# Attention weights turned in pairs of 64-row tiles, eight blocks a visit, with the first scores head by head

## The chip, the cores and the metric

The kernel runs on one core of a Trainium2 chip. The metric is the device time of one execution in microseconds (us), lower is better. The engines speak here by their names in the profile: PE (TensorE, the matmul array) with PEld (its weight loads), DVE (VectorE), ACT (ScalarE), POOL and SP (the queue that issues most DMA).

## The reference

Three stages over 4 batch entries of 576 positions and 512 features, all float32.

```python
def _attn_ref(q, k, v):              # (4, 8, 576, 64): 8 heads of 64
    q_rot, k_rot = rotate(q), rotate(k)
    scores = q_rot @ k_rot.T / np.sqrt(64)
    attn = np.exp(scores - scores.max(-1, keepdims=True))
    attn = attn / (attn.sum(-1, keepdims=True) + 1e-9)
    return attn @ v
def _moe_ref(x, g_ln, w_ch1, w_ch2): # 512 -> 2048 -> 512
    xn = (x - mu) / np.sqrt(var + 1e-6) * g_ln
    return x + np.maximum(xn @ w_ch1, 0) @ w_ch2
def _moe2_ref(x, w_in, g_ln, w_sg, b_sg, w_out):
    u, v = split(gelu(x @ w_in))     # 512 -> 1024
    v_s = w_sg @ layernorm(v) * ... + b_sg    # mixes the 576 positions
    return x + (u * v_s) @ w_out
```

## The kernel before

**Groups, blocks, units.** A group is one batch entry (g = 0 to 3). A block is a pair of heads (p = 0 to 3) of a group and a part `hi` of its query positions: `hi` = 0 holds 384 of them, `hi` = 1 the other 192. A unit is up to 128 query positions of a block: three full units for `hi` = 0; one full unit and one single unit of 64 positions for `hi` = 1 (`PARTS`, L20). Group 0 takes the four blocks of `hi` = 0 first and then the four of `hi` = 1; the other groups alternate.

**One unit** (`Attn.unit`, L258). Scores S for 576 keys go into two PSUM areas, S[0] and S[1], one a head, two banks each. In a full unit head j lies on array rows 64j to 64j+63, so the two heads' matmuls (K = 64, 288 columns, L271) use different row halves of the array. A single unit has both heads' 64 queries side by side as 128 (tile `qd`), with all 128 rows. DVE takes the row maxima (L293), ACT the exp with its sum (L303) into the tile P (128 queries by 1152 keys of both heads).

**Turning P** (`turn`, L317, and `evac`, L340). P is needed with keys on partitions, so blocks of 128 by 128 are transposed by the array (L334), three to a visit, into one of two PSUM tiles T of one bank each, and copied to the SBUF tile PT by ACT or DVE (L347; L352 and L356 for a single unit). Which of the two copies is decided when the program is built (L343, with `EVEN`). A full unit has 9 blocks, a single one 5.

**P V** (`values`, L382). When all of a block's PT stands, chunk 4 of the keys (64 keys of each head in one zero-padded 128-row tile) goes over the full array (L394), then chunks 0 to 3 head by head in column halves (64 array columns each, L398). It takes a T tile; the reciprocal sums, spread by `scale` (L364), are transposed into another (L408). ACT copies P V to the tile x0 (L410), and DVE multiplies (L415, L419).

**LayerNorm and MLP.** `ln` (L491) and `rest` (L517) run when all four pairs of a half (group 0) or of a group are there; group 0 normalises half 0 and half 1 apart. `ln` has its mean's matmul in a T tile (L508), `rest` its variance's in an MLP bank (L549; for groups 1 to 3 with 64 of the columns of `ones`, so that both halves lie in one tile). The MLP steps `up` (L644) and `down` (L671) have six matmuls of 288 columns each and use two more PSUM banks (`mps`, counted by `mpsb`). Weights come as doubles and are split by `convert` (L614) on ACT and DVE during group 0. For half 0 alone, `group0` (L732) offers four up and four down steps of pass 0 and two up steps of pass 1. After the MLP of group 3 the second block, `moe2` (L895), runs; no line of it changes.

**The order** of each engine's work is written out when the program is built: `Sched` (L64) keeps a clock for each engine, asks every task when its next step can start and how long the step takes, takes the earliest start and among equals the lowest rank (`RANK`, `UNIT`, `NORM`, `REST`); a task of lower rank that can start within `HOLD` of the chosen step's length goes ahead of it (L100). The MLP has rank 5. The numbers of this planner decide the order only; the waits are semaphores.

Of the kernel before, what the change touches and what calls it, by code (L numbers as in the profile page):

```python
# [15 lines left out]
HQ = 288  # L16
# [47 lines left out]
class Sched:  # L64
# [7 lines left out]
    def __init__(self):  # L72
        self.e = dict.fromkeys(("PE", "DVE", "ACT", "POOL", "SP"), 0.0)
        self.tasks = []
        self.n = 0

# [6 lines left out]
    def go_on(self, t, end):  # L83
        try:
            t["eng"], t["at"], t["us"], *rank = t["gen"].send(end)
# [6 lines left out]
    def run(self, until=lambda: False):  # L92
        while self.tasks and not until():
# [41 lines left out]
class Attn:  # L135
# [10 lines left out]
    def __init__(self, tc, ctx, k, groups, sched):  # L146
# [5 lines left out]
        self.T, self.qin, self.kin, self.vfree, self.K = Bank(2), Bank(QB), Bank(2), Bank(2), Bank(KB)  # L152
# [105 lines left out]
    def unit(self, i):  # L258
# [3 lines left out]
        x0 = (g, B["p"])  # L262

        heads = range(2 if m == 128 else 1)
        for n in range(2):
            yield "PE", (lambda: latest(*self.Sfree, Kb["k"], B["q"], self.k["x0_free"](*x0))) if n == 0 else 0.0, 0.57
# [5 lines left out]
            self.Sfree = [None, None]  # L272
        e = c.e["PE"]
        if u["t"] == 0:
            self.k["x0"](*x0)
        if u["last"]:
            self.qin.give(B["qslot"], e + 0.1)
            if B["hi"]:
                self.QD.give(B["dslot"], e + 0.1)
            Kb["kusers"] -= 1  # L280
            if Kb["kusers"] == 0:
                self.K.give(Kb["kslot"], e + 0.1)
        if i + 1 < len(self.units):
            c.task(self.unit(i + 1), UNIT[self.units[i + 1]["g"]])
        if u["t"] == 0:
            self.ahead(B["n"])
            B["su"] = self.p.tile([128, 6], F32, tag="su", name="su", bufs=3)
            B["left"] = 0
        at = []
        nb = self.p.tile([128, 2], F32, tag="nb", name="nb", bufs=3)  # L290
        for j in heads:
            e = yield "DVE", e + 0.35 if j == 0 else 0.0, 0.77
            nc.vector.tensor_reduce(nb[:, j:j + 1], S[j], AX.XY, ALU.max, negate=True)  # L293
            at.append(e + 0.1)
        P = None
        u["P"] = []
        for j in heads:
            e = yield "ACT", (lambda: latest(at[0], self.P.free())) if j == 0 else at[j], 0.97
            if j == 0:
                slot = self.P.take()  # L300
# [5 lines left out]
            if len(heads) == 1:  # L306
                self.Sfree[1] = e + 0.05
# [823 lines left out]
```

## Time and profile before

| | |
|---|---|
| median of 3 runs | 948.84 us (948.66 to 951.78) |
| the profiled execution | 947.07 us, its span 945.3 us |
| PE busy | 916.1 us (97%) |
| DVE, ACT busy | 638.3 us (68%), 490.9 us (52%) |
| granted PE clock | 9 or more tenths in all slices |

The page gives each engine's busy time, and digits for 40 equal slices of the span (23.6 us each; a digit is the busy share in tenths, 9 is 90% or more). Matmuls overlap on PE, so the sum of their durations is more than its time; the distance between starts tells what one costs. In the timeline a row is: start, time until the end of the last of the merged instructions, engine, line, operation, out<-in, rows*columns of the array used, shape of the moving operand, and count. A float32 matmul appears as two instructions, a transpose as one.

### The profile page before, as it was taken

Reading aid. Unit: us, or ns where it says so; the run is one execution under the profiler, and the core shown is the slowest. Engines: PE = TensorE matmul, PEld = TensorE weight load, DVE = VectorE, ACT = ScalarE, POOL = GpSimd, SP = SyncE. Lnnn points to the kernel's source line nnn. Section 1 sums busy time; section 2 is a strip of 40 time slices with the busy share of each in tenths; the row PEclk is TensorE's granted clock in tenths of the full one; section 3 lists DMA queues with packets and bytes.
Section 4 is the critical chain, followed back from the end, with each engine's and each line's share of the span. In section 5 each row is a group of like instructions: output and inputs, shape, how many; then the busy total and the mean of one; then the engine's idle time right before and its main releaser. Section 6 shows DMA issues by size and latency. Waiting matters only on the chain.

```text
span 945.3 us, 16622 instructions
## 1 busy us (share of the span) xinstructions
PE 916.1 (97%) x6448; PEld 799.5 (85%) x6448; DVE 638.3 (68%) x1353; ACT 490.9 (52%) x1191; POOL 0.8 (0%) x9
## 2 busy tenths in 40 slices
PE   4889999999999999999999999989999999999998
PEld 2446878788788787899877899989999999999998
DVE  6799887887869744825767423674534898676754
ACT  2688787778654755524255413444322656263530
POOL 0000000000000000000000000000000000000000
PEclk9999999999999999999999999999999999999999
DMA  6477616674536055225730453878752201202011
GB/s 205 167 239 242 218 43 199 220 249 172 201 110 206 18 182 182 84 74 184 230 114 22 131 163 98 304 238 295 247 190 80 84 1 31 83 1 88 1 51 51
DMA packets 57791, 134.69 MB, mean 142 GB/s; under 512 B 8048, under 2 KB 30448, under 8 KB 57712
## 3 DMA queue, kind: packets, MB, share of 16 engines
q1 hardware_dynamic: 56880, 132.96, 42.5%
q8 instruction: 51, 0.84, 0.4%
q10 hardware_dynamic: 832, 0.66, 0.3%
q14 instruction: 28, 0.23, 0.1%
HBM read 106.50 MB, written 26.21 MB: 140 GB/s over the span
## 4 chain that ended last, share of the span: by engine, by line
PE 93%; DVE 3%; ACT 2%; DMA 1%; issue 1%; SPq 0%; DVEq 0%
PE S L271 9%; PE T L334 8%; PE m L686 7%; PE m L685 7%; PE m L687 7%; PE m L655 7%; PE PV L398 7%; PE m L656 7%; PE m L657 7%; PE PV L394 2%; PE p L964 2%; PE p L962 2%; PE p L963 2%; PE p L1062 2%; PE p L1046 2%; PE p L1061 2%
## 5 line engine op out<-in xcount | busy, mean ns | idle before, releaser
L655 PE MATMUL m<-xh,w 128*128 128x288 f32 x480 | 147.1, 306 | 3.5 <-DVE h L665 3.5
L685 PE MATMUL m<-h,w 128*128 128x288 f32 x480 | 146.0, 304 | 0.0
L686 PE MATMUL m<-h,w 128*128 128x288 f32 x480 | 141.8, 295 | 0.0
L656 PE MATMUL m<-xl,w 128*128 128x288 f32 x480 | 141.6, 295 | 0.0
L657 PE MATMUL m<-xh,w 128*128 128x288 f32 x480 | 141.2, 294 | 0.0
L687 PE MATMUL m<-h,w 128*128 128x288 f32 x480 | 140.5, 293 | 0.0
L303 ACT ACTIVATE P<-S,nb 128x576 f32<-128x576 f32 x144 | 106.4, 744 | 42.4 <-DVE nb L293 39.3
L665 DVE SCALAR_TENSOR_TENSOR h<-m,h 128x288 fp32r<-128x288 f32 x128 | 58.1, 455 | 100.5 <-ACT h L663 99.4
L293 DVE TENSOR_REDUCE nb<-S 128x1 f32<-128x576 f32 x144 | 103.6, 752 | 26.4 <-PE S L271 25.8
L334 PE MATMUL T<-ident,P 128*128 128x128 f32 x656 | 100.1, 280 | 9.0 <-ACT P L303 4.9
L347 ACT COPY PT<-T 128x384 f32<-128x384 f32 x157 | 70.7, 483 | 69.4 <-PE T L334 69.2
L334 PEld LDWEIGHTS T<-ident,P 128*128 128x128 f32 x656 | 74.9, 141 | 37.3 <-issue 12.7
L663 ACT ACTIVATE h<-m 128x288 fp32r<-128x288 f32 x128 | 52.5, 410 | 100.2 <-PE m L657 98.7
L271 PE MATMUL S<-K,qin 64*128 64x288 f32 x512 | 85.2, 439 | 11.0 <-DVE K L205 11.0
L655 PEld LDWEIGHTS m<-xh,w 128*128 128x128 f32 x480 | 90.1, 188 | 5.8 <-DVE h L665 4.2
L685 PEld LDWEIGHTS m<-h,w 128*128 128x128 f32 x480 | 90.1, 188 | 0.8 <-DVE acc L709 0.4
L686 PEld LDWEIGHTS m<-h,w 128*128 128x128 f32 x480 | 90.4, 188 | 0.4
L656 PEld LDWEIGHTS m<-xl,w 128*128 128x128 f32 x480 | 90.3, 188 | 0.2
L657 PEld LDWEIGHTS m<-xh,w 128*128 128x128 f32 x480 | 90.3, 188 | 0.0
L687 PEld LDWEIGHTS m<-h,w 128*128 128x128 f32 x480 | 90.1, 188 | 0.0
L271 PEld LDWEIGHTS S<-K,qin 64*128 64x128 f32 x512 | 47.7, 190 | 31.1 <-DVE K L205 11.0
L398 PE MATMUL PV<-PT,vin 128*64 128x384 f32 (+1 forms) x512 | 70.3, 413 | 0.0
(148 smaller groups left out, 1797.3 us busy)
## 6 DMA issues: line engine op xcount, KB each, us to landing
w<-wsc SPq DMA_DIRECT2D x96, 512.0 KB, 4.0
cd<-in_w SPq DMA_DIRECT2D x32, 512.0 KB, 4.3
wsc<-w SPq DMA_DIRECT2D x24, 512.0 KB, 4.2
kin<-in_k SPq DMA_DIRECT2D x15, 576.0 KB, 5.9
vin<-in_v SPq DMA_DIRECT2D x20, 320.0 KB, 3.9
qin<-in_q SPq DMA_DIRECT2D x16, 384.0 KB, 5.2
x1d<-x SPq DMA_DIRECT2D x32, 144.0 KB, 3.3
x<-x1d SPq DMA_DIRECT2D x32, 144.0 KB, 2.8
```

Of the source, the lines that this page charges most:

```text
L271: nc.tensor.matmul(S[j][:, n, :], q, Kb["K"][r, a:a + HQ], start=True, stop=True)
L293: nc.vector.tensor_reduce(nb[:, j:j + 1], S[j], AX.XY, ALU.max, negate=True)
L303: nc.scalar.activation(P[:, 576 * j:576 * j + 576].rearrange("p (n k) -> p n k", n=2), S[j], AF.Exp, bias=nb[:, j:j + 1], scale=1.0, accum ...
L334: nc.tensor.transpose(ps[:, 128 * n:128 * n + 128], P[:, 128 * i:128 * i + 128], self.k["ident"])
L347: copy(t[:, 3 * k:3 * k + 3, q0:q0 + 128], ps[:, 0:384].rearrange("p (c q) -> p c q", c=3))
L398: nc.tensor.matmul(ps[r, 0:n], V["vin"][:, ch, r], t[:, 5 * j + ch, 0:n], start=False, stop=ch == 3, skip_group_check=True)
L655: nc.tensor.matmul(ps, w[:, 0, ms], xh[:, kc, :], start=kc == 0, stop=False)
L656: nc.tensor.matmul(ps, w[:, 0, ms], xl[:, kc, :], start=False, stop=False)
L657: nc.tensor.matmul(ps, w[:, 1, ms], xh[:, kc, :], start=False, stop=kc == 3)
L685: nc.tensor.matmul(ps, w[:, 0, ms], t[:, 0, :], start=a == 0, stop=False)
L686: nc.tensor.matmul(ps, w[:, 1, ms], t[:, 0, :], start=False, stop=False)
L687: nc.tensor.matmul(ps, w[:, 0, ms], t[:, 1, :], start=False, stop=a == n - 1)
```

## The change

`turn` becomes a task of a whole block: it goes through all 128 by 128 blocks of P of the block's units, eight to a visit (in group 0's `hi` = 0 blocks four or five). A block of P is turned by two transposes, of rows 0 to 63 and 64 to 127, each 64 columns wide, in different row halves of the array and into different banks. T becomes one tile of two banks. `evac` copies each unit's part of a visit in one instruction. `values` takes all chunks in column halves, chunk 4 too, each with its own head's 64 columns of V; P V and the reciprocals lie in the two banks of one T tile, or for group 0's `hi` = 0 in two of the MLP's banks. There too the heads of a unit are tasks of their own in `unit`, and the chunks of P V are single steps. The variance's matmul in `rest` uses all 128 columns of `ones`. `Sched` knows three modes of PE (full, "r" for row tiles, "c" for column tiles) and adds 0.2 to a step that changes the mode, after having chosen it. The ranks and `EVEN` have new numbers.

```diff
-UNIT = [2, 1, 3, 2.5]
-EVEN = [0, 9, 3, -1]
-RANK = dict(turn=4.5, evac=1.25, values=2.25, end=-1, convert=2.75, prep=3.5, load=4, loader=4)
-NORM, REST = [2.25, 0, 3.5, 1.25], [0.25, 4.5, 1, 1]
+SWITCH = 0.2
+ALONE = ((0, 0),)
+UNIT = [1.75, 1.75, 3, 3.5]
+EVEN = [9, 1, 1, 0]
+RANK = dict(end=-1, convert=2.5, prep=2.75, load=4.5, loader=4)
+NORM, REST = [0.25, 0.25, 2.75, 1.75], [1.75, 1.75, 3.5, 4.5]
+TURN, EVAC, VAL = [2, 0.5, 1.25, -1], [1.5, 0.25, 1.5, 2.5], [2, 1.5, 0.5, 0.75]
...
+            if t["eng"] == "PE":
+                if t["mode"] != self.mode:
+                    t["us"] += SWITCH
+                self.mode = t["mode"]
...
-        self.T, self.qin, self.kin, self.vfree, self.K = Bank(2), Bank(QB), Bank(2), Bank(2), Bank(KB)
+        self.T, self.qin, self.kin, self.vfree, self.K = Bank(), Bank(QB), Bank(2), Bank(2), Bank(KB)
...
-    def unit(self, i):
+    def unit(self, i, heads=None):
...
-        heads = range(2 if m == 128 else 1)
+        if heads is None:
+            heads = (0, 1) if m == 128 and (g, B["hi"]) not in ALONE else (0,)
...
+        after = single or heads[-1] == 1
+        if not after:
+            c.task(self.unit(i, (1,)), UNIT[g])
...
-    def turn(self, u, P, slot, at):
+    def turn(self, B, units):
...
-        for k in range(3 if full else 2):
-            need = 1 if full and k else 0
...
-            ps = self.ps.tile([128, 512], F32, tag="T", name="T", bufs=2)
-            for i in range(3 * k, 3 * k + 3):
...
-                nc.tensor.transpose(ps[:, 128 * n:128 * n + 128], P[:, 128 * i:128 * i + 128], self.k["ident"])
+        blocks = [(u, i) for u in units for i in range(9 if u["m"] == 128 else 5)]
+        cuts = [0]
+        while cuts[-1] < len(blocks):
+            u, i = blocks[cuts[-1]]
+            cuts.append(min(cuts[-1] + (8 if (B["g"], B["hi"]) not in ALONE else 5 if i or u["m"] < 128 else 4), len(blocks)))
+        for v, z in zip(cuts, cuts[1:]):
+            some = blocks[v:z]
...
+            self.T.take()
+            ps = self.ps.tile([128, 2, 512], F32, tag="T", name="T")
+            for n, (x, i) in enumerate(some):
+                for j in range(2):
+                    r = slice(64 * j, 64 * j + 64)
+                    nc.tensor.transpose(ps[:, j, 64 * n:64 * n + 64], x["tile"][r, 128 * i:128 * i + 128], self.k["ident"][r, r])
...
-            copy(t[:, 3 * k:3 * k + 3, q0:q0 + 128], ps[:, 0:384].rearrange("p (c q) -> p c q", c=3))
+                copy(t[:, i:i + n, q0:q0 + 128].rearrange("p c (j q) -> p j c q", j=2),
+                     ps[:, :, 64 * s:64 * s + 64 * n].rearrange("p j (c q) -> p j c q", q=64))
...
-                nc.tensor.matmul(ps[:, 0:n], V["vin"][:, 4, :], t[:, 4, 0:n], start=True, stop=False, skip_group_check=True)
-            for ch in (2 * s, 2 * s + 1):
+                if early:
+                    bank = self.k["mpsb"].take()
+                    ps = self.k["mps"].tile([128, 512], F32, tag="m", name="PV")
+                else:
+                    self.T.take()
+                    both = self.ps.tile([128, 2, 512], F32, tag="T", name="PV")
+                    ps, pb = both[:, 0, :], both[:, 1, :]
+            for ch in chs:
                 for j in range(2):
                     r = slice(64 * j, 64 * j + 64)
-                    nc.tensor.matmul(ps[r, 0:n], V["vin"][:, ch, r], t[:, 5 * j + ch, 0:n], start=False, stop=ch == 3, skip_group_check=True)
+                    nc.tensor.matmul(ps[r, 0:n], V["vin"][:, ch, r], t[:, 4 if ch == 4 else 5 * j + ch, 0:n], start=ch == 0, stop=ch == 4)
...
-        ps = mps.tile([128, 512], F32, tag="m", name="ln")[a:a + m, 0:HQ]
+        ps = mps.tile([128, 512], F32, tag="m", name="ln")[:, 0:HQ]
...
-            nc.tensor.matmul(ps, ones[:, 0:m], x, start=i == 0, stop=i == len(xs) - 1)
+            nc.tensor.matmul(ps, ones, x, start=i == 0, stop=i == len(xs) - 1)
```

## Rows read from the trace of the kernel before

**Rows 1.** The page: busy time of each engine, then PE by slices.

```profile
PE 916.1 (97%) x6448; PEld 799.5 (85%) x6448; DVE 638.3 (68%) x1353; ACT 490.9 (52%) x1191; POOL 0.8 (0%) x9
...
PE   4889999999999999999999999989999999999998
```

**Rows 2.** Stretches: window, length, PE, PEld, DVE, ACT, POOL, clock, DMA.

```profile
11.00:79.00 68.00, 58.44 (x318) 33.23 (x319) 59.35 (x109) 47.63 (x111) 0.00 (x0) 1.00 0.59 196
79.00:640.00 561.00, 555.49 (x4019) 474.15 (x4019) 381.02 (x811) 313.44 (x794) 0.00 (x0) 1.00 0.49 161
640.00:945.30 305.30, 302.14 (x2114) 292.08 (x2112) 194.12 (x428) 128.33 (x286) 0.00 (x0) 1.00 0.28 91
```

**Rows 3.** Timeline of PE: full-array S and six transposes among MLP matmuls.

```profile
166.81 0.30 PE L657 MATMUL m<-xh,wx 128*128 128x288 f32 x1
166.94 1.13 PE L271 MATMUL S<-K,qd 128*128 128x288 f32 x4
167.91 0.82 PE L334 MATMUL T<-ident,P 128*128 128x128 f32 x6
168.49 0.38 PE L655 MATMUL m<-xh,wx 128*128 128x288 f32 x1
168.71 0.29 PE L656 MATMUL m<-xl,wx 128*128 128x288 f32 x1
```

**Rows 4.** Timeline of PE: a paired S and six transposes behind it.

```profile
123.64 0.30 PE L657 MATMUL m<-xh,wx 128*128 128x288 f32 x1
123.86 1.24 PE L271 MATMUL S<-K,qin 64*128 64x288 f32 x8
125.03 0.88 PE L334 MATMUL T<-ident,P 128*128 128x128 f32 x6
125.67 0.38 PE L655 MATMUL m<-xh,wx 128*128 128x288 f32 x1
```

**Rows 5.** Timeline of PE: P V of 192 columns and what follows it.

```profile
104.75 0.49 PE L394 MATMUL PV<-PT,vin 128*128 128x192 f32 x2
105.17 1.52 PE L398 MATMUL PV<-PT,vin 128*64 128x192 f32 x16
106.62 1.24 PE L271 MATMUL S<-K,qd 128*128 128x288 f32 x4
```

**Rows 6.** Loads of that S and T; when PE's queue reached T's wait.

```profile
123.86 0.18 PEld L271 LDWEIGHTS S<-K,qin 64*128 64x128 f32 x1 [0.17 <-issue]
123.86 0.19 PEld L271 LDWEIGHTS S<-K,qin 64*128 64x128 f32 x2 [0.17 <-issue]
125.03 0.14 PEld L334 LDWEIGHTS T<-ident,P 128*128 128x128 f32 x1 [0.38 <-issue]
125.09 0.25 PEld L334 LDWEIGHTS T<-ident,P 128*128 128x128 f32 x2
...
L334 PEldq EVENT_SEMAPHORE  x1: 51/51/51, 123.6 to 123.6; - x1
```

**Rows 7.** Instructions of tile T by stretches: PE, PEld, DVE, ACT, clock, DMA.

```profile
11.00:79.00 68.00, 19.34 (x117) 12.98 (x117) 6.55 (x12) 11.89 (x26) 1.00 0.59 196
79.00:640.00 561.00, 80.74 (x539) 61.93 (x539) 15.80 (x37) 73.88 (x213) 1.00 0.49 161
```

**Rows 8.** Groups by line, forms apart: ACT's copy out of T.

```profile
L347 ACT COPY PT<-T 128x384 f32<-128x384 f32 x157 | 70.7, 483 | 69.4 <-PE T L334 69.2
```

**Rows 9.** Waits of PE from 11 to 79 us: total, times, longest.

```profile
PE T L334 <- ACT P L303: 4.7, 4, 1.5
PE T L334 <- DVE PT L347: 2.2, 4, 0.7
PE T L334 <- ACT PT L347: 1.3, 5, 0.3
```

**Rows 10.** The chain that ended last: matmuls of group 0's two LayerNorms.

```profile
78.91 2.06 PE ln L508 x8
119.87 2.14 PE ln L508 x8
```

More of the change, by code (lines that the diff above doesn't have):

```diff
@@ L262, in unit @@
         x0 = (g, B["p"])
-        heads = range(2 if m == 128 else 1)
+        if heads is None:
+            heads = (0, 1) if m == 128 and (g, B["hi"]) not in ALONE else (0,)
+        single = m == 64
         for n in range(2):
-            yield "PE", (lambda: latest(*self.Sfree, Kb["k"], B["q"], self.k["x0_free"](*x0))) if n == 0 else 0.0, 0.57
+            yield "PE" if single else "PEr", (lambda: latest(*(self.Sfree[j] for j in ((0, 1) if single and (g, B["hi"]) not in ALONE else heads)), Kb["k"], B["q"],
+                                                             self.k["x0_free"](*x0))) if n == 0 else 0.0, 0.49
             for j in heads:
@@ L271, in unit @@
                 nc.tensor.matmul(S[j][:, n, :], q, Kb["K"][r, a:a + HQ], start=True, stop=True)
-            self.Sfree = [None, None]
+                self.Sfree[j] = None
         e = c.e["PE"]
[L274 to L290, printed above, removed]
+        if heads[0] == 0:
+            if u["t"] == 0:
+                self.k["x0"](*x0)
+                self.ahead(B["n"])
+                B["su"] = self.p.tile([128, 6], F32, tag="su", name="su", bufs=3)
+                B["left"] = 0
+                B["turned"] = False
+            u["P"], u["at"] = [], []
+            u["nb"] = self.p.tile([128, 2], F32, tag="nb", name="nb", bufs=3)
@@ new lines, in unit @@
+        after = single or heads[-1] == 1
+        if not after:
+            c.task(self.unit(i, (1,)), UNIT[g])
+        if after:
+            if u["last"]:
+                self.qin.give(B["qslot"], e + 0.1)
+                if B["hi"]:
+                    self.QD.give(B["dslot"], e + 0.1)
+                Kb["kusers"] -= 1
+                if Kb["kusers"] == 0:
+                    self.K.give(Kb["kslot"], e + 0.1)
+            if i + 1 < len(self.units):
+                c.task(self.unit(i + 1), UNIT[self.units[i + 1]["g"]])
@@ L299, in unit @@
             if j == 0:
-                slot = self.P.take()
-                P = self.p.tile([128, 1152], F32, tag="P", name="P", bufs=PB)
+                u["slot"] = self.P.take()
+                u["tile"] = self.p.tile([128, 1152], F32, tag="P", name="P", bufs=PB)
+            P = u["tile"]
             s = 2 * u["t"] + j
@@ L305, in unit @@
             self.Sfree[j] = e + 0.05
-            if len(heads) == 1:
-                self.Sfree[1] = e + 0.05
-            if j == 0:
-                c.task(self.turn(u, P, slot, at), RANK["turn"])
-            if len(heads) == 1:
+            if j == 0 and u["t"] == 0:
+                c.task(self.turn(B, [x for x in self.units if x["B"] is B]), TURN[B["g"]])
+            if single:
                 e = yield "ACT", 0.0, 0.2
@@ L403, in values @@
         at = e
-        f = yield "PE", lambda: latest(B.get("inv"), self.T.free()), 0.08 + 0.00087 * n
-        b2 = self.T.take()
-        pb = self.ps.tile([128, 512], F32, tag="T", name="inv", bufs=2)
+        f = yield "PE", lambda: latest(B.get("inv"), free() if early else 0.0), 0.08 + 0.00087 * n
+        if early:
+            bank2 = self.k["mpsb"].take()
+            pb = self.k["mps"].tile([128, 512], F32, tag="m", name="inv")
         for i in range(3 if B["hi"] == 0 else 2):
@@ L555, in rest @@
         r = G[g, "r"]
[L556 removed]
+        nc.scalar.copy(r[a:a + m], ps[a:a + m])
         mpsb.give(bank, e + 0.05)
```

110 lines of the change are left out of this document (61 added, 49 removed).

## The prediction

> **What bounds the kernel now.** I read the head of the page first: TensorE is busy 916.1 of 945.3 us, and its digits are lowest in the first three slices [rows 1]. The table by stretches then cuts the span in three [rows 2]. Up to 79 us there is no MLP to fill gaps: TensorE is busy 58.44 of the 68 us after 11, VectorE 59.35. From 79 to 640 us TensorE is busy 555.49 of 561. The tail after 640 us holds no line of the diff. So between 79 and 640 us every us of TensorE's time is a us of the span; before 79 us the end of the stretch is set by a chain over three engines. The granted clock is 1.00 in all of them, which is 2.4 GHz.
>
> A busy matmul is not its price, since matmuls overlap. The price is the distance from one start to the next, read in the timeline. After six transposes the first MLP matmul starts 0.58 us behind the first of them (167.91 to 168.49), and the matmul behind that one comes 0.22 us later instead of 0.13. So six blocks cost 0.58 + 0.09 = 0.67, **0.11 us a block** (0.109 in the sums below, within the rounding of these starts), and a visit among MLP matmuls has no further price [rows 3].
>
> Half-array work has one. Eight instructions of a paired S visit stand in four pairs, as long as the four of a full-array S: yet the full one lets T start 0.97 us behind it (166.94 to 167.91) and the paired one 1.17 (123.86 to 125.03). That is 0.20 for emptying the array. Entering costs 0.22 - 0.13 = 0.09 (123.64 to 123.86), and six T behind a paired S take 0.64 instead of 0.58, another 0.06 [rows 3, 4]. So one **change-over into row tiles and back is about 0.35 us**. The column tiles of P V pay the same kind of price: two full-array instructions of 192 columns take 0.42 us (104.75 to 105.17), though each pair of the sixteen behind them takes at most 1.45/8 = 0.18 [rows 5].
>
> **The change, part by part.**
>
> **1. A block as two 64-row transposes.** 656 blocks stay 656 blocks, but each becomes two instructions that stream 64 columns instead of 128. Are halves run side by side, their loads too? In S they are: two loads of different row groups together take 0.19 us, and the first alone 0.18 [rows 6]. The matmul half is then half of 0.109, or 0.055. The load: the second T load starts 0.06 behind the first (125.03, 125.09) [rows 6]. I take 0.057 a pair, so 0.052 saved. No row shows a 64-column pair of transposes, so I bound it: 0.053 where the columns alone decide, and 0.18 at the other end, the spacing of the densest pairs of the trace [rows 5], which their 192 columns explain. I stay at the low end because S shows the same row tiles side by side. After 79 us there are 539 of the 656 blocks [rows 7]: 539 x 0.052 = **28.0 us less**.
>
> **2. More visits in row tiles.** By the code, a block of three full units has 27 blocks to turn, cut in four visits (8, 8, 8, 3); the second halves have 14, in two. After 79 us that makes 12 x 4 + 16 x 2 = 80 visits. A visit next to a paired S shares its change-over; one that stands alone pays 0.35. At least 28 stand alone: the fourth of each of 12 blocks, and the first of 16 second halves, whose next S is the full-array one. The T area is now one tile of two banks in place of two tiles, and P V holds it from its first matmul until VectorE has scaled the result, so a T visit waits behind that and comes after its S. I take half, 40 x 0.35 = **14 us more**; 28 would be 10, all 80 would be 28.
>
> **3. Copies out of the T area.** Fewer and longer. Today 26 on ScalarE take 11.89 and 12 on VectorE 6.55 us up to 79 us [rows 7]. They stand beside TensorE's MLP work after 79 us and cost nothing there; ScalarE and VectorE are busy 313 and 381 of 561 us [rows 2]. If that cover went, the wait would be one copy, some 0.48 x 8/3 = 1.3 us at most a visit [rows 8]. Only the next T visit is behind it on TensorE, and `mlp` steps fill in.
>
> **4. Up to the first LayerNorm.** The twelve first S visits split by head: 24 half visits of four instructions in one row group, each as long as a full-array S, 0.97 us, against 12 x 1.17. That is 23.3 - 14.0 = 9.3 us more for TensorE. 108 transposes save 108 x 0.052 = 5.6. So TensorE gets 3.7 us more, in a stretch where the sum of its starts-to-starts (14.0 + 108 x 0.109 + four P V of some 4, twice the 1.87 us of 192 columns [rows 5]) is 42 of 68 us: idle time hides it. What the split gives: the first reduction can start 0.97 us after S instead of 1.17, and the next S of a head waits only for that head's exp. TensorE's waits for ScalarE's P sum to 4.7 us and for copies of PT to 3.5 here [rows 9]. P V leaves the T area for the MLP's banks, which nobody uses yet. Its copies fall from 36 to 24 of 4 or 5 blocks; at 0.48 for 3 blocks, 0.64 for 4 and 0.80 for 5 if the time goes wholly by columns, they cost some 24 x 0.65 = 15.6 against 17.5 (36 of the 38 copies that sum to 18.44 [rows 7]). The pieces of the chain that the trace shows give no exact figure. The bounds: 10 us shorter (TensorE's 8.2 us of named waits gone, and 1.9 of copies) to 6 longer (the 3.7 us, and some change-overs between P V's single steps and S). I take **3.5 us less**, nearer to the waits than to the extra S because idle time covers the latter.
>
> **5. Between the two LayerNorms of group 0.** The LayerNorm matmuls start at 78.91 and 119.87 [rows 10]. In between only half 0's MLP can fill in: eight steps of pass 0 and two of pass 1, ten x 12 matmuls x 0.133 = 16 us. The four second halves now go through one T area: two visits, their copies, P V and the scaling one after another, some 10 us a block (P V 1.9 [rows 5], two visits with copies of about 2 each, inv, copy and scaling some 1.7 by the 0.48 of a copy, and the rest of an MLP step of 0.8 ahead of each). 4 x 10 is about the 41 us of today, while TensorE has some 2.9 us less to do in it (4 x 14 x 0.052). I charge **2 us**; 0 to 6.
>
> **6. Small ones.** The six LayerNorm visits of 64 columns become full-array: 6 x some 0.25 = **1.5 us less** (the change-over above less the step behind S). Chunk 4 in column tiles streams as many columns, two at once, as it did in one: 0, since the change-over inside P V only moves to its front; at best its 0.09 goes 28 times, 2.5 us. The new ranks I count at nothing: after 79 us they permute work that TensorE must do anyway, and before it they are inside the bounds of 4 and 5. No DMA is moved by hand; the loads of K, Q and V are asked for blocks ahead on SP's queue, as before.
>
> The **sum**: -28.0 + 14.0 - 3.5 + 2.0 - 1.5 = -17.0 us. The profiled execution took 947.07 us, its span 945.3; the median of the runs shown is 948.84, 1.8 above it. So 947.07 - 17.0 = **930.1 us**.
>
> **The rivals.**
>
> *A. Halves do not come fast enough (slower).* If the two loads of a pair follow one another, a pair costs 2 x 0.057 = 0.114: 539 x 0.005 = 2.7 more in place of 28 less, and the time is 947.07 + 2.7 + 11.0 = 961. The other terms sum to +11.0, so the point from which it decides is 0.109 - 11.0/539 = 0.089 us a pair. Against it: the loads of S side by side [rows 6], and that TensorE's queue had reached T's wait at 123.6 while T's first load came at 125.03, so instructions stand ready [rows 6]. For it: nothing in the trace starts two matmuls per 0.057 us for long. A rule of the Trainium skill speaks for it (TensorE: Matmul & The Clock Gate, section "Wait — 56ns, not 53.3ns?"): with hardware decode off the sequencer spends about 62 ns on each matmul, which binds once the array needs less. By that, as an estimate, a pair would cost 0.124 us and the sum would be 947.07 + 8.1 + 11.0 = 966; the densest matmuls here stand at 0.09 each, so no run shows it. Chance 0.08.
>
> *B. One T area makes every visit stand alone, and the LayerNorm of half 1 late.* 80 x 0.35 = 28 eats all of part 1; nothing won up to the first LayerNorm, 4 us lost in 5: 947.07 - 28 + 28 - 1.5 + 4 = 949.6. For it: P V's hold on the area; against: S becomes ready at the same exp that T waits for. Chance 0.10.
>
> *C. The chain up to the first LayerNorm was the larger cost.* Ten us there, nothing lost in 5, and only the 28 forced visits alone: 947.07 - 28 + 10 - 10 - 1.5 = 917.6. For it: 26 of 68 us idle there. Against: VectorE is busy 59 of the 68. Chance 0.15.
>
> **How the numbers follow.** The forecast has 0.67, with 921 to 942 as its own range. Down to 914 takes in C; up to 944 the upper bounds of part 2. Left out are A and B, 0.18. A measurement of this kernel can tell 0.5%, 4.7 us. Faster by more: the forecast, C and a little of B, 0.83. Within: most of B and the forecast's edge, 0.09. Slower: A, 0.08.
>
> **What would show it.** In the timeline after, eight blocks (16 transposes) should lie about 0.46 us from first start to last, and the MLP matmul behind them some 0.3 us later than it would without a change-over; 0.9 would be A. The LayerNorm's first matmul should start near 75 us, the second near 117. Between 79 us and the end of the attention, the stretch should be some 15 us shorter with the same MLP matmuls. I am wrong in part 2 if transposes stand next to S nearly always or never, and in part 4 if the first LayerNorm moves by more than 10 us.

## The result, and the profile after

The changed kernel takes 937.42 us (median of 4 runs, 936.17 to 939.15) against 949.35 for the kernel before in the same set (4 runs, 948.66 to 951.78): a ratio of **0.9871, 95% interval 0.9844 to 0.9898**. The profiled execution took 936.35 us with a span of 934.6, so 10.7 less than the 947.07 on which the sum was made; forecast were 17.0 less. The sign was right, the size was missed by 6.3.

The head of the page of after, to be read against [rows 1]: PE's second and third digits are 9 where they were 8, the fourth 8 where it was 9.

```profile
PE 908.4 (97%) x7168; PEld 788.5 (84%) x7168; DVE 618.8 (66%) x1306; ACT 500.7 (54%) x1142; POOL 0.8 (0%) x9
...
PE   4998999999999999999999999999999999999998
```

**Where the time went.** The best cut is not the one at 79 us of [rows 2] but a point of equal MLP work. The table by stretches for the tile m (the MLP's matmuls; columns: window, length, PE busy and count, clock, DMA) shows 132 of them done in both kernels when `rest` of half 1 of group 0 starts (the second variance matmuls, "the second rest" below). First before, then after:

```profile
0.00:129.60 129.60, 20.76 (x132) 1.00 0.59 199
```

```profile
0.00:131.62 131.62, 20.66 (x132) 1.00 0.54 184
```

Up to there the changed kernel is **2.0 us later**, from there to the end 12.7 us shorter (802.98 us against 815.72). The two rows of the tile T from there on, before and after:

```profile
129.58:945.30 815.72, 70.56 (x474) 1.00 0.41 133
```

```profile
131.62:934.60 802.98, 43.01 (x932) 1.00 0.41 138
```

There are 474 blocks left before and 465 after (930 halves start there; the row's 932 counts two that are still running), so after is 9 blocks ahead, and also one paired S visit (400 S instructions left against 408). Busy time is no price here, since matmuls overlap. So I summed the distances from one PE start to the next over the timeline, from the second rest to the last run of matmuls of the second block (my sums):

| start to start, us | before | after | difference |
|---|---|---|---|
| T | 48.17 | 34.93 | -13.2 |
| MLP matmuls, with the longer step behind a change-over | 406.99 | 413.11 | +6.1 |
| S paired | 53.22 | 50.04 | -3.2 |
| S of single units | 11.66 | 13.60 | +1.9 |
| P V without the reciprocals | 64.63 | 61.84 | -2.8 |
| LayerNorm matmuls | 8.30 | 6.96 | -1.3 |
| reciprocals | 7.65 | 7.45 | -0.2 |
| second block | the same | the same | 0.0 |
| sum | | | -12.7 |

**One visit**, answering [rows 3]. Timeline of PE in after, a visit of eight blocks alone among MLP matmuls:

```profile
120.30 0.29 PE L732 MATMUL m<-h,w 128*128 128x288 f32 x1
120.52 0.71 PE L355 MATMUL T<-ident,P 64*128 64x64 f32 x16
121.16 0.40 PE L730 MATMUL m<-h,w 128*128 128x288 f32 x1
121.40 0.30 PE L731 MATMUL m<-h,w 128*128 128x288 f32 x1
```

Sixteen halves take 0.64 us from their first start to the next MLP matmul. Within the visit, from the second pair on, a pair starts every 0.0625 us (the loads of a pair lie 1 to 6 ns apart, the next pair's 0.060 to 0.063 us behind). Eight pairs are 0.50. Three parts are left: the rest of the 0.64, which is 0.14; the step of 0.24 instead of 0.13 behind the first MLP matmul; and the step of 0.22 instead of 0.13 ahead of T. They sum to **0.34 us** for the change-over of a visit that stands alone.

**P V**, answering [rows 5], where 192 columns took 1.87 us, from 104.75 until 106.62: with all chunks in column tiles it is 1.77 us from the first start to the next instruction.

```profile
207.58 0.29 PE L732 MATMUL m<-h,w 128*128 128x288 f32 x1
207.80 1.85 PE L437 MATMUL PV<-PT,vin 128*64 128x192 f32 x20
209.57 0.44 PE L448 MATMUL PV<-ident,rb 128*128 128x128 f32 x2
```

**The start.** The table by stretches of after, its first window, answers the first line of [rows 2]: PE busy 65.02 us of 68 in place of 58.44, and still the first LayerNorm is later, 81.73 against 78.74 us. The group of its line gives the first and the last start behind the three durations. The second LayerNorm begins at 116.5, against 119.8 [rows 10].

```profile
11.00:79.00 68.00, 65.02 (x460) 40.85 (x462) 48.42 (x89) 46.84 (x104) 0.00 (x0) 1.00 0.42 145
```

```profile
L553 PE MATMUL ln<-x,ones x16: 406/406/481, 81.7 to 118.0; 128*128 128x288 f32 x16
```

Of the 8.2 us of waits of [rows 9], 2.9 are left; from 11 to 81 us PE waits 2.1 us for P and 0.8 for PT:

```profile
PE S L283 <- ACT P L320: 2.1, 2, 1.5
PE T L355 <- ACT PT L379: 0.8, 1, 0.8
```

So PE has become the bound of the start, and the timeline tells why. The same instructions start at twice the distance up to 39.7 us as behind it:

```profile
35.41 0.68 PE L283 MATMUL S<-K,qin 64*128 64x288 f32 x1
...
35.89 0.68 PE L283 MATMUL S<-K,qin 64*128 64x288 f32 x1
...
37.04 1.55 PE L437 MATMUL PV<-PT,vin 128*64 128x384 f32 x4
...
40.56 1.51 PE L437 MATMUL PV<-PT,vin 128*64 128x384 f32 x8
...
42.70 0.40 PE L283 MATMUL S<-K,qin 64*128 64x288 f32 x1
...
42.95 0.40 PE L283 MATMUL S<-K,qin 64*128 64x288 f32 x1
```

Four P V instructions take 1.55 us at 37 us and eight take 1.51 at 40.6; two S starts are 0.48 us apart and then 0.25. That is TensorE at its lower level (1.2 GHz) and at its upper one (2.4 GHz). The trace's granted clock rises at 39.7 us. The clock column of the window above shows 1.00 all the same: it has nothing to report before the first recorded change. PE is busy all of the 20 us from 20 to 40 (the row below), with S of one head at a time on one half of the array's rows, pairs of 64-row transposes, and the first P V, four matmuls at 32.81 and four at 37.04; the rise follows. In the kernel before, whose timeline stands below that row, the step lies at 19.5 us: six transposes take 1.54 us at 18.04 there (0.82 in [rows 3]) and three 0.55 at 20.89.

```profile
20.00:40.00 20.00, 20.00 (x107) 1.00 0.43 155
```

```profile
18.04 1.54 PE L334 MATMUL T<-ident,P 128*128 128x128 f32 x6
20.89 0.55 PE L334 MATMUL T<-ident,P 128*128 128x128 f32 x3 [1.30 <-ACT P L303]
```

### The profile page after: what moved, and what is told of

Its sections match the earlier page's. It is cut to its first block, busy times and chain, and to the rows that moved or that the text cites. A ratio compares the mean times of both kernels' runs of the same rounds, so it can differ in the third digit from the quotient of the medians.

```text
span 934.6 us, 17884 instructions
## 1 busy us (share of the span) xinstructions
PE 908.4 (97%) x7168; PEld 788.5 (84%) x7168; DVE 618.8 (66%) x1306; ACT 500.7 (54%) x1142; POOL 0.8 (0%) x9
## 4 chain that ended last, share of the span: by engine, by line
PE 94%; ACT 2%; DVE 2%; DMA 1%; issue 0%; SPq 0%; DVEq 0%
PE S L283 9%; PE PV L437 9%; PE m L730 8%; PE m L700 8%; PE m L731 7%; PE m L732 7%; PE m L701 7%; PE m L702 7%; PE T L355 6%; PE p L1009 2%; PE p L1007 2%; PE p L1008 2%; PE p L1089 2%; PE p L1107 2%; PE p L1106 2%; PE p L1090 2%
## 5 line engine op out<-in xcount | busy, mean ns | idle before, releaser
L283 PE MATMUL S<-K,qin 64*128 64x288 f32 x512 | 99.7, 451 | 14.2 <-DVE K L214 11.0
L379 ACT COPY PT<-T 128x1024 f32<-128x1024 f32 (+3 forms) x126 | 78.4, 641 | 64.2 <-PE T L355 63.8
L700 PEld LDWEIGHTS m<-xh,w 128*128 128x128 f32 x480 | 90.0, 187 | 12.1 <-issue 5.4
L437 PE MATMUL PV<-PT,vin 128*64 128x384 f32 (+1 forms) x640 | 88.5, 417 | 1.4 <-ACT PT L390 1.3
L283 PEld LDWEIGHTS S<-K,qin 64*128 64x128 f32 x512 | 56.1, 201 | 32.4 <-DVE K L214 11.0
L355 PEld LDWEIGHTS T<-ident,P 64*128 64x128 f32 x1312 | 57.3, 142 | 27.5 <-issue 11.9
L355 PE MATMUL T<-ident,P 64*128 64x64 f32 x1312 | 72.7, 234 | 4.1 <-ACT PT L379 1.9
```

Source lines behind the costliest of these rows:

```text
L283: nc.tensor.matmul(S[j][:, n, :], q, Kb["K"][r, a:a + HQ], start=True, stop=True)
L355: nc.tensor.transpose(ps[:, j, 64 * n:64 * n + 64], x["tile"][r, 128 * i:128 * i + 128], self.k["ident"][r, r])
L379: copy(t[:, i:i + n, q0:q0 + 128].rearrange("p c (j q) -> p j c q", j=2), ps[:, :, 64 * s:64 * s + 64 * n].rearrange("p j (c q) -> p j c q ...
L437: nc.tensor.matmul(ps[r, 0:n], V["vin"][:, ch, r], t[:, 4 if ch == 4 else 5 * j + ch, 0:n], start=ch == 0, stop=ch == 4)
L700: nc.tensor.matmul(ps, w[:, 0, ms], xh[:, kc, :], start=kc == 0, stop=False)
```

## The experiments

The theory at first: pairs of halves and their visits account for the gain, and the split by head for what was lost or won at the start. Its rivals: TensorE's level at the start; the ranks; the P V banks; the size of a visit. All kernels stand in one table, from their traces and times. A ratio is to the kernel before in the same set, whose median lay between 947.3 and 949.4 us, so differences of some 2 us between medians of different sets say little. "Lower level" is the time at 1.2 GHz from 11 us to the second rest, by the granted clock; it can have cost PE half of itself at most.

| kernel | median us | ratio to before (95%) | first, second LayerNorm, second rest us | lower level us |
|---|---|---|---|---|
| before | | | 78.7, 119.8, 129.6 | 8.5 |
| after | 937.42 | 0.9871 (0.9844 to 0.9898) | 81.7, 116.5, 131.6 | 28.7 |
| before, heads split | 971.90 | 1.0242 (1.0218 to 1.0266) | 92.6, 144.8, 156.5 | 36.3 |
| heads together | 957.99 | 1.0097 (1.0062 to 1.0132) | 82.2, 130.1, 146.9 | 28.0 |
| warm-up | 937.72 | 0.9892 (0.9870 to 0.9914) | 81.4, 117.8, 132.9 | 27.3 |
| full rows | 939.10 | 0.9902 (0.9882 to 0.9922) | 77.4, 117.9, 132.8 | 10.9 |
| old ranks | 971.93 | 1.0246 (1.0221 to 1.0272) | 100.9, 150.8, 157.7 | 58 |
| whole blocks | 970.44 | 1.0232 (1.0207 to 1.0256) | 92.7, 131.0, 143.4 | 32.4 |
| four a visit | 986.14 | 1.0398 (1.0369 to 1.0428) | 84.2, 169.5, 187.0 | 56 |
| P V in T | 996.54 | 1.0499 (1.0472 to 1.0526) | 123.1, 172.6, 190.9 | 107 |
| full rows, ranked | 932.03 | 0.9830 (0.9806 to 0.9854) | 78.5, 113.6, 125.7 | 10.3 |
| heads together, ranked | 939.99 | 0.9908 (0.9884 to 0.9933) | 78.2, 121.0, 129.5 | 25 |
| whole blocks, ranked | 966.03 | 1.0168 (1.0134 to 1.0202) | 101.0, 139.2, 153.0 | 56 |
| P V in T, ranked | 951.97 | 1.0036 (1.0019 to 1.0053) | 92.1, 133.3, 143.7 | 54 |

**Heads together** (the split by head undone, ranks of after):

```diff
-            heads = (0, 1) if m == 128 and (g, B["hi"]) not in ALONE else (0,)
+            heads = (0, 1) if m == 128 else (0,)
```

> The changed kernel with one part undone: in group 0's first four blocks both heads of a unit are one S visit again (paired row tiles), all else as changed. Theory 1 (TensorE's rate): in the changed kernel S pairs of one head stand 0.48 us apart until 39.7 us and 0.24 after, in the kernel before only until 19.5; what TensorE does before the rise is half-array work with one head at a time. With the heads together the spacing should fall to 0.24 by about 20 to 25 us, group 0's first LayerNorm matmul should start near 75 us instead of 81.7, and the time should be about 931 us (6 less than the changed kernel's 937.4). Theory 2 (the split helps the chain, and something else holds the stretch): the first LayerNorm stays at 81 us or later and the time at 937 or above.

Measured: 957.99. That misses theory 1; the LayerNorm and the time lie where theory 2 put them, but 20 us are far more than it explains. The level rises at 18.6 us, as theory 1 said, but falls back four times before the second rest, and the first LayerNorm comes at 82.2 all the same. PE now waits for copies and exps (waits of PE from 11 to 82 us):

```profile
PE T L355 <- ACT PT L379: 6.6, 9, 0.8
PE T L355 <- ACT P L320: 4.5, 3, 1.5
```

Half 0's MLP steps are used up before the second LayerNorm: from 124.9 to 150.3 us no MLP matmul starts. Either the split is worth 20 us or after's order doesn't fit a kernel without it; this run can't tell.

**Warm-up** (30 full-array matmuls of 128 columns while the first K is awaited):

```diff
+    warm = mps.tile([128, 512], F32, tag="m", name="warm")
+    for i in range(30):
+        nc.tensor.matmul(warm[:, 0:128], ones, ones, start=True, stop=True)
```

> The changed kernel with work added: 30 full-array matmuls of 128 columns on a constant tile into an MLP bank nobody reads, in TensorE's idle first 11 us. Theory 1: the first S then runs at the full rate. If half-array work with one head at a time keeps the rate up, S pairs stand 0.24 us apart from 11 us on, the first LayerNorm starts near 74 us, and the time is about 930. If that work does not keep it, the rate falls back to 0.48 within some us and the time stays at 937. Theory 2 (the rate is no cause): S may run faster, but the LayerNorm stays at 81 us and the time at 937.

Measured: 937.72, no gain; both theories allow that time. The timeline shows that TensorE does start at the upper level and then loses it in the split scores:

```profile
11.21 1.49 PE L283 MATMUL S<-K,qin 64*128 64x288 f32 x8 [0.48 <-DVE K L214]
...
17.59 1.32 PE L283 MATMUL S<-K,qin 64*128 64x288 f32 x2 [0.82 <-ACT P L320]
```

Eight S take 1.49 us, then two take 1.32. The granted clock is low again from 17.1 to 41.0 us. So the late rise isn't that of a cold start: in this run the split scores lose a level that was already there.

**Before, heads split** (the split alone, in the kernel before, old ranks; main lines):

```diff
-        heads = range(2 if m == 128 else 1)
+        if heads is None:
+            heads = (0, 1) if m == 128 and (g, B["hi"]) != (0, 0) else (0,)
...
+        if not after:
+            c.task(self.unit(i, (1,)), UNIT[g])
```

> The kernel before with one part of the change alone: in group 0's first four blocks the two heads of a unit are S visits of their own (one row group at a time); turning, P V and ranks as before. Theory (one-head S keeps TensorE at the half rate): instead of at 19.5 us the rise to the full rate comes after 30 us, and the first LayerNorm matmul, at 78.7 us before, does not come sooner: 78 to 84 us; the time 948 to 955. Rival (splitting the heads shortens the chain as I forecast, the half rate of the changed kernel has another cause): rise before 25 us, first LayerNorm near 74, time near 943.

Measured: 971.90, 24.6 us slower than before and above the expected 948 to 955. The level rises at 44.1 us instead of 19.5: eight S right behind it take 1.25 us, the eight P V ahead of it 2.61.

```profile
41.88 2.61 PE L405 MATMUL PV<-PT,vin 128*64 128x384 f32 x8
44.42 1.25 PE L273 MATMUL S<-K,qin 64*128 64x288 f32 x8
```

The split alone brings the late rise, without paired transposes. The first LayerNorm is 13.9 us later.

**Old ranks** (after with before's numbers; TURN, EVAC and VAL as constants 4.5, 1.25, 2.25):

```diff
-UNIT = [1.75, 1.75, 3, 3.5]
-EVEN = [9, 1, 1, 0]
+UNIT = [2, 1, 3, 2.5]
+EVEN = [0, 9, 3, -1]
...
```

> The changed kernel with the numbers of the planner from before: UNIT, EVEN, RANK, NORM, REST as they were, the turns, copies and P V with their old ranks 4.5, 1.25 and 2.25. My prediction counted new ranks at nothing: then 934 to 942. Rival (four blocks a visit cost 49 us and joined heads 16, nearly all between group 0's two LayerNorms, where half 0's MLP steps run out; the order there is what the new ranks bought): the second LayerNorm later than 120 us and the time 945 or more.

Measured: 971.93, 34.5 us above after. 26.1 of the 35 us of the profiled runs lie ahead of the second rest. The table by stretches shows the level, since here the clock column has changes to report:

```profile
40.00:70.00 30.00, 23.84 (x160) 15.65 (x160) 20.64 (x39) 21.22 (x44) 0.00 (x0) 0.73 0.50 176
70.00:100.00 30.00, 24.76 (x156) 12.73 (x154) 21.30 (x41) 19.32 (x40) 0.00 (x0) 0.76 0.63 219
```

The granted clock is 0.73 and 0.76. The 29 us more at the lower level than in after can have cost 14.6 at most; of the other 11 or more, PE's waits from 11 to 100 us name 7.7 for copies of PT and 5.1 for P. That is the rival's case.

**Whole blocks** (full-array transposes of 128 columns in the same visits, ranks of after; main lines):

```diff
-                for j in range(2):
-                    r = slice(64 * j, 64 * j + 64)
-                    nc.tensor.transpose(ps[:, j, 64 * n:64 * n + 64], x["tile"][r, 128 * i:128 * i + 128], self.k["ident"][r, r])
+                nc.tensor.transpose(ps[:, n // 4, 128 * (n % 4):128 * (n % 4) + 128], x["tile"][:, 128 * i:128 * i + 128], self.k["ident"])
```

> The changed kernel with one part undone: each 128 by 128 block is turned by one full-array transpose again, in the same visits of eight (or four and five), the same two banks and the same ranks. Theory 1 (the gain is the pair): each of 656 blocks costs 0.109 instead of the 0.0625 us that the changed kernel's trace shows, 30.5 us back; the visits no longer change the array's mode, some 30 that stand alone after the second LayerNorm and about 8 before save 0.34 each, 13 us; in sum about 937.4 + 17 = 955 us. Rival (larger visits and new ranks are what gained): 937 to 942.

Measured: 970.44, 33 us above after and 15 above what the theory gave. Both the price of a block and an order laid out for another price are in it.

**Four a visit** (four blocks in place of eight):

```diff
-            cuts.append(min(cuts[-1] + (8 if (B["g"], B["hi"]) not in ALONE else 5 if i or u["m"] < 128 else 4), len(blocks)))
+            cuts.append(min(cuts[-1] + (4 if (B["g"], B["hi"]) not in ALONE else 5 if i or u["m"] < 128 else 4), len(blocks)))
```

> The changed kernel with one size changed: four blocks a visit instead of eight outside group 0's first blocks. After the second LayerNorm the visits go from 72 to 132. Theory (a visit that stands alone pays 0.34 us to change the array's mode and back): with half of the 60 new ones alone, 30 x 0.34 = 10 us more, 947 us; all alone 20 us, 957. Rival (change-overs are covered, what counts is the transposes): 937 to 940.

Measured: 986.14, beyond even the 957 of all visits alone. Behind the second rest the timeline has 112 stretches in row tiles against 71 in after. From each start to the next there I took off the distance that the same instructions keep back to back; what is left sums to 59.7 us against 45.5 in after (my sums). That is 14.2 us for 41 more stretches, **0.35 us each**: the price of a change-over from another side. What makes the kernel 49 us slower than after lies ahead of the second rest, which comes at 187.0 against 131.6 us. Some 20 of these 55 us are work that after does only behind it (55 blocks, seven S visits and three P V among it), and the level, low for 24 us from 84 us on, can have cost 12 more. From 127.6 to 180.0 us no MLP matmul starts, so nothing fills in when T waits for a copy at visit after visit (waits of PE from 84 to 187 us):

```profile
PE T L355 <- ACT PT L379: 7.5, 10, 1.2
PE PV L437 <- ACT PT L390: 2.2, 2, 1.3
PE ln L553 <- ACT PT L379: 2.0, 2, 1.2
```

**P V in T** (the first blocks' P V in the T area, ranks of after):

```diff
-        early = (B["g"], B["hi"]) == (0, 0)
+        early = False
```

> The changed kernel with one part undone: P V of group 0's first four blocks is written to the T area instead of the MLP's idle banks. If the T area is what the first stretch waits for, the first LayerNorm comes 4 or more us later than 81.7 and the time is 941 or more; if TensorE itself is the bound there (it waits for nothing but 2.9 us after 11 in the changed kernel), the LayerNorm stays within 2 us and the time at 936 to 939.

Measured: 996.54, 59 us above after, with the first LayerNorm at 123.1 and 107 us at the lower level. That is the first case of the expectation, the T area as what the start waits for; but again the order is one made for another kernel.

**Full rows** (the first scores head by head, but over all 128 rows, with the other head's Q zeroed; ranks of after; main lines):

```diff
-                r = slice(64 * j, 64 * j + 64) if m == 128 else slice(0, 128)
-                q = B["Q"][r, 0, q0:q0 + 128] if m == 128 else self.qd[B["dslot"]]
+                r = slice(64 * j, 64 * j + 64) if m == 128 and (g, B["hi"]) not in ALONE else slice(0, 128)
+                q = B["Q"][r, j if (g, B["hi"]) in ALONE else 0, q0:q0 + 128] if m == 128 else self.qd[B["dslot"]]
```

> The changed kernel with one part replaced: in group 0's first four blocks each head's S runs over all 128 rows, with the other head's rows of Q set to zero (two adds of half the rows on VectorE instead of one, two memsets on GpSimd); one head at a time as in the changed kernel, four instructions a visit, and no change of the array's mode. Theory (the half rate until 39.7 us comes from half-array work and costs TensorE about 10 us there): the rise comes by about 20 us, the first LayerNorm near 74 to 77 us instead of 81.7, the time near 931. Rival (one head at a time is slow whatever the rows): the rise stays at 35 us or later or the LayerNorm at 81, the time at 937.

The edit adds three zero fills on POOL (two of Q, one of K) and one more addition on DVE to each of the first blocks; the instructions on PE are as many and as long. Measured: the level rises at 15.1 us, as the timeline shows (eight S in 3.74 us, then four in 1.24), and the first LayerNorm comes 4.3 us earlier than in after, at 77.4.

```profile
11.97 3.74 PE L295 MATMUL S<-K,qin 128*128 128x288 f32 x8 [11.97 <-POOL qin L247]
15.95 1.24 PE L295 MATMUL S<-K,qin 128*128 128x288 f32 x4 [0.24 <-ACT P L332]
```

But the whole takes 939.10, no better than after and 8 us above the theory. The gain is given back between the LayerNorms. There PE stands idle several times in front of the second halves' transposes and P V, its level falls (table by stretches: granted clock 0.76), and a P V of 192 columns takes 3.47 us instead of 1.85:

```profile
77.40:91.50 14.10, 11.04 (x76) 7.88 (x77) 11.21 (x26) 10.98 (x28) 0.00 (x0) 0.76 0.81 281
```

```profile
81.45 0.71 PE L367 MATMUL T<-ident,P 64*128 64x64 f32 x16 [0.68 <-DVE xc L569]
83.31 0.86 PE L367 MATMUL T<-ident,P 64*128 64x64 f32 x12 [1.14 <-ACT PT L391]
85.38 3.47 PE L449 MATMUL PV<-PT,vin 128*64 128x192 f32 x20 [1.22 <-ACT PT L402]
```

That settles the cause of the late rise, not its whole price. And the runs so far kept an order that was made for another kernel. The last four give four of them ranks of their own, chosen by the planner's clock, all from UNIT to VAL.

**Full rows, ranked** (the edit of full rows, and):

```diff
+UNIT = [1.25, 1.75, 1.75, 3.5]
+EVEN = [2, 9, 0, 1]
+RANK = dict(end=-1, convert=2.25, prep=2.75, load=0.5, loader=4)
+NORM, REST = [0, 1.5, 3, 0.75], [1.25, 2, 0.75, 4.5]
+TURN, EVAC, VAL = [1.25, 0.75, -1, 3.5], [-1, 0.5, -1, -1], [2, 0.75, 1.5, 1]
```

> The full-rows kernel (each head's S of group 0's first blocks over all 128 rows with the other head's Q rows zero) with ranks of the planner chosen anew for it; the changed kernel's ranks were fitted to its own steps. Theory (in the full-rows kernel the first LayerNorm came 4.3 us sooner, and an order that did not fit it gave the gain back): the rise to the full rate by 20 us, the first LayerNorm at 78 us or sooner, and 930 to 934 us, below the changed kernel's 937.4. Rival (the half rate of the first 40 us is hidden anyway): 937 or more.

Measured: **932.03**, the lowest median of all; its five runs (931.1 to 933.8) lie below the four of after (936.2 to 939.2). The two ratios are closer, 0.9830 and 0.9871, and their intervals overlap by 0.001. The profiled run is the slowest of the five, 2.5 us below the profiled one of after. The second rest comes at 125.67 us, 6.0 earlier than in after (chain that ended last):

```profile
113.55 2.18 PE ln L565 x8
...
125.67 1.94 PE ln L606 x8
```

**Heads together, ranked** (main lines of the ranks):

```diff
+UNIT = [0.75, 1.75, 1.25, 3]
+EVEN = [3, 3, 2, 3]
...
+TURN, EVAC, VAL = [1, 0.25, -1, 2.75], [-1, 0.25, 0.25, 1.5], [1.5, 1.5, 1, 1.75]
```

> Both heads of a unit in one S visit throughout, ranks chosen anew for that. Run with the changed kernel's ranks it took 953 to 962 us. Theory (an order fitted to another structure lost most of that; the split itself is worth little, since it holds TensorE at the half rate): 932 to 938 us. Rival (the split by head is worth some 16 us): 945 or more.

Measured: 939.99, 18 us better than with after's ranks, and between the theory's 932 to 938 and the rival's 945. By that the split is worth 2.6 us, which is not clear of the noise: the intervals of the two ratios overlap. With the heads together the level rises early (19.3), but PE then waits for P (4.8 us from 20 to 39) and loses the level for short times, five times before 88 us.

**Whole blocks, ranked:**

```diff
+UNIT = [1.75, 1.75, 0.5, 1.25]
+EVEN = [3, 5, -1, 5]
...
+TURN, EVAC, VAL = [1.75, 2.25, 2, 3], [1, 1, 1, 3], [2, 0.5, 3, 1.5]
```

> Whole-block transposes over the full array in the visits of eight, ranks chosen anew for that. Run with the changed kernel's ranks it took 970 us. Theory: pairs save 656 x 0.0465 = 30.5 us and their change-overs after the second LayerNorm take some 9 back, so about 937.4 + 21 = 958 at most, and less as far as the new order also mends the first stretch: 948 to 958. Rival (the pair is worth the whole 33 us that the first run showed): 965 or more; rival (pairs are worth less than 5): below 943.

Measured: 966.03, 28.6 above after, close to the 33 of the run with after's ranks. The time is the first rival's, but its cause isn't. The row of T from the second rest on, to be read against the 802.98 us of after:

```profile
152.99:964.30 811.31, 63.85 (x468) 1.00 0.41 135
```

There it takes 811.3 us, with 468 blocks against 465 in after. That is what pairs are worth to PE-bound work there, each kernel with its own order: **8.3 us net**, 12.3 less between T's starts (47.18 against 34.93) and 4 back, in change-overs above all. The other 21.4 us lie ahead of it, where the level rises only at 63.4 us. The timeline just ahead of the rise and behind it:

```profile
59.97 2.83 PE L436 MATMUL PV<-PT,vin 128*64 128x384 f32 x8
...
66.49 0.87 PE L436 MATMUL PV<-PT,vin 128*64 128x384 f32 x4
```

How much of the 21.4 is the level and how much the longer transposes on a bound PE isn't separated; 27 us more at the lower level bound the first at 13.5.

**P V in T, ranked:**

```diff
+UNIT = [1.25, 1.75, 3, 3.5]
+EVEN = [0.5, 0.5, 3, 3]
...
+TURN, EVAC, VAL = [1.25, 1.75, 2.25, 1.25], [0, 1.25, 1.25, 0.75], [1.25, 0.5, 1.25, 0.75]
```

> P V of group 0's first blocks in the T area, ranks chosen anew for that. Run with the changed kernel's ranks it took 997 us. Theory (most of those 59 us were an order that did not fit): 940 to 948, so the MLP's banks are worth 3 to 10 us. Rival (the one T area cannot serve P V and turns in the first stretch): 960 or more.

Measured: 951.97. The MLP's banks for the first P V are worth 14.5 us, more than the few expected and far from the 59 of the run with after's ranks. 12.1 of the profiled 15.6 lie ahead of the second rest. Without them the whole first P V comes later, and with it the rise, at 48.3 us; two more stretches at the lower level follow (table by stretches):

```profile
40.00:70.00 30.00, 28.94 (x157) 16.34 (x156) 18.17 (x38) 18.31 (x39) 0.00 (x0) 0.83 0.36 117
70.00:93.00 23.00, 19.08 (x138) 12.12 (x138) 17.99 (x36) 17.04 (x35) 0.00 (x0) 0.85 0.63 211
```

## Why the prediction was right, and where it wasn't

The sum of -17.0 splits at the second rest. Behind it lie 474 blocks (-24.6), 72 of the 80 visits (12.6) and the LayerNorm's visits (-1.5): -13.5 predicted, **-12.7 measured**. That is closer than the parts deserve: 9 blocks and one S visit, some 2.1 us at the old prices, had been done before the cut, so like for like it is about -10.6. Between the first LayerNorm and the second rest: 65 blocks (-3.4), 8 visits (1.4) and part 5 (2.0), together 0; measured -1.0 (50.9 us before, 49.9 after). Up to the first LayerNorm -3.5 predicted, **+3.0 measured**. The misses are 0.8, -1.0 and 6.5, in sum the 6.3.

- **What bounds the kernel**: right for everything behind the LayerNorms of group 0, where the table of distances closes, and PE's waits from 132 to 640 us sum to 5.5 us. Wrong for the start in one point: the clock column of [rows 2] was read as 2.4 GHz, while TensorE was at the lower level until 19.5 us. The doubled durations of the first transposes would have shown it.
- **Part 1, the pair**: right. 0.0625 us, between the 0.053 estimated for the columns alone and the 0.18 of the far bound, by 0.0055 above the 0.057 taken: by that 539 blocks save 25.1, not 28.0. **Rival A falls**: its point is 0.089. With it goes the rule of the Trainium skill that was set beside it (TensorE: Matmul & The Clock Gate, section "Wait — 56ns, not 53.3ns?", some 62 ns on each matmul with hardware decode off): two matmuls per 0.0625 us, sixteen in a row, are 31 ns each, so this trace doesn't agree with it as a bound here; which way matmuls are decoded no run shows. The lower bound that the same section states, about 25 ns from start to start, holds here on the average alone: the two halves of a pair start 3 to 5 ns apart (120.518 and 120.521 us for the first).
- **Part 2, the visits**: right in price (0.34 alone in the timeline, 0.35 by the four-block run, 0.35 taken). By count the forecast was half the visits alone; behind the second rest the timeline has 27 T visits alone and 41 next to a paired S. But those 41 don't share it wholly: row stretches are 71 against 46, and 3 S visits stand alone. T, MLP and S together give -8.4, of which some 2.1 is the work already done (9 blocks, one S visit). The 465 pairs save 21.6, so 15.3 are left for change-overs and waits, where 12.6 were forecast; the 25 stretches more than before, by 0.34, are 8.5 of it. The remaining 7 are not assigned row by row. That a change of mode empties the array is also what the Trainium skill states (TensorEngine Tiling (Array Packing), section "Key Properties"); it gives no price, and the trace's is 0.34. **Rival B** falls with it: not every visit is alone, and the second LayerNorm comes at 116.5, where 117 was forecast. It does so with 30 fewer MLP matmuls done (72 against 102), so its time alone says little.
- **Part 3, copies**: right where the MLP covers them. PE's waits from 132 to 640 us name no copy of PT. The copy of eight blocks takes 1.02 us (ACT's row at 121.27), under the 1.3 worked out from [rows 8]. Where nothing covers them, in the start of heads together (6.6 us) and with four blocks a visit (7.5), they are the largest wait.
- **Part 4, the first LayerNorm**: the step that failed, and by its sign. Most of its named waits did go, 5.3 of the 8.2 us [rows 9]. What failed is "idle time hides it": the 42 us of PE work in 68 were priced at the upper level. With one head at a time on half the rows the lower level lasts to 39.7 us instead of 19.5, PE is busy 65 of 68 us, and it is PE that is late. The split in the kernel before brings the late rise by itself (44.1), full rows take it away (15.1, first LayerNorm 4.3 us earlier), and a warm-up doesn't. The 20 us more at the lower level than before bound its cost at 10, against the 6.5 missed; how much of the 6.5 it is, no run separates. **Rival C** falls for this kernel; with full rows the first LayerNorm came 1.3 us before that of the kernel before (77.4 against 78.7), and nowhere 10.
- **Part 5**: right within its bounds.
- **Part 6**: the LayerNorm visits give -1.3, where -1.5 was forecast. Chunk 4 isn't nothing: -2.8 over 24 visits, 0.12 each, a little over its stated best case of 2.5. **Ranks at nothing was wrong**: the old ones cost 34.5 us, and of the 34.9 by which the profiled spans differ 8.8 lie behind the second rest, where "they permute work that TensorE must do anyway" (some 2 of the 8.8 are 11 blocks and an S visit that after had done before). The order decides how many change-overs there are (82 row stretches behind the second rest with the old ranks, 71 in after) and whether half 0's MLP lasts until half 1's LayerNorm (with the old ranks no MLP matmul starts from 142.6 to 155.3 us). The time was inside the range only because the new ranks came with the change.

Open is how much of after's time the lower level costs. Full rows with new ranks win 5.4 us with 18 us less of it, but the ranks were changed together with it, and no run has new ranks in after with nothing else changed; so a part of the 5.4 may be the ranks'. Nor does a run give the kernel before ranks chosen anew, so what the new order alone is worth stays open; that the blocks themselves cost less is seen apart from it, in the distances between T's starts.

## What to carry to other kernels

Row-tiled pairs of transposes do run side by side here, at 0.0625 us a block in place of 0.109. Change-overs of 0.35 us a visit take a good part of that back (4 of 12.3 us against whole blocks in visits of eight), so put as much into one visit as PSUM holds, and put it next to work that is row-tiled anyway. Where a kernel starts with matmuls on part of the array, one at a time, look at their durations against those of the same instruction later in the trace: that an engine is busy doesn't show at which level it runs. And where an order is written out by ranks, a kernel with one part undone and another's ranks measures the ranks too: four runs here moved by 4 to 45 us when theirs were fitted.

## What the runs showed of the hardware

- How the array was used, and not only whether it was busy, went with TensorE's level in these fourteen kernels. It rose at 15.1 to 17.9 us with the first scores over all rows, at 18.6 to 19.5 with both row halves at once, and at 36.8 to 63.4 with one half at a time, in after with PE busy 20.00 of the 20 us from 20 to 40. After 30 full-array matmuls it was up at 6.8 and fell at 17.1, in the one-half scores. With one half at a time the rise (in the warm-up kernel its second) came 3.8 to 24.8 us behind the first P V matmul, in the five other kernels 7.9 to 14.7 us ahead of it; these distances are from the clock's recorded changes to PE's starts.
- In before and after the clock column says 1.00 ahead of the first recorded change, though the level was the lower one. S of 288 columns took 0.68 us there and 0.40 behind it.
- Matmuls of 64 columns in two row halves start 31 ns apart on average, fourteen in a row behind the first pair: 3 to 5 ns within a pair, 0.0625 us from pair to pair.
- A column-tiled P V of 192 columns with no full-array part in front took 1.77 us against 1.87, and 24 of them, of both lengths, 2.8 us less.
